# A gated scan and two feed-forward networks on one core: the scan steps of a pair of blocks released at given TensorE steps, planned in finer pieces, with a planner that may wait shortly for a step

## The chip, the cores and the metric

One core of a Trainium2 chip. The metric is the device time of one execution in microseconds (us).

## The reference

```python
sig = 1.0 / (1.0 + np.exp(-f_logit))                 # batch 2, sequence 6080, width 256
f = lower_bound + (1.0 - lower_bound) * sig
for t in range(S):                                   # per batch, from h = 0
    h = f[:, t] * h + (1.0 - f[:, t]) * x[:, t]
    y[:, t] = h
x = y.reshape(B * S, D)                              # 12160 tokens
h = np.maximum(x @ w_in, 0.0); x = h * h @ w_out     # network 1, hidden width 2048
h = x @ w_in2; g = np.where(h > 0, h, np.exp(np.minimum(h, 0)) - 1)
out = g @ w_out2                                     # network 2, hidden width 2048
```
The weights arrive as float64 and are brought to float32 on the chip.

## The kernel before, in words

**Blocks and slots.** The 12160 tokens are cut into 24 blocks (the first of 384 tokens, the others of 512), taken two by two as pairs. For one network, one block and one of 8 groups of 256 hidden units there is one *slot* of work, 384 slots in all. Network 1 of one pair (16 slots) alternates with network 2 of the pair two places earlier (16 slots). Counted from 0, slots 0 to 31 are network 1 of the first two pairs, 32 to 47 network 2 of the first pair, 48 to 63 network 1 of the third pair, 64 to 79 network 2 of the second pair, and so on: a *cycle* has 32 slots.

**One slot.** float32 products are made of three rounded ones (a value is split into a rounded high part and its residual). TensorE does `first` (3 of 7 block products of the input side, L611), then the output products of the slot three before (`out`, L710), then `later` (the other 4, L611). ScalarE copies three quarters of the PSUM result to SBUF (`snap`, L639) between `first` and `later`. VectorE adds the pieces (L647, L654, L642, L650), ScalarE takes the first block (L657) and the activation: relu and square for network 1; for network 2 two steps L667 and L670, after which VectorE forms the elu (L673). ScalarE rounds the result (L678), VectorE makes its residual (L683, tile `g`): this is the last thing that `out` of the slot waits for. In the text "the residual of slot 64" is that slot's L683. The first four blocks of network 1 use plain products (L625) instead of L611.

**The scans.** Each block is scanned in two halves, each a chain of steps: two loads on the SP queue (`fs`, `xs`), a tanh on ScalarE (L545), on VectorE two transposes (L550), the gate (two instructions L559), the scan's input (L562), the scan itself (two instructions L576) and the copy of the last column for the next half (L578). The buffers `fs`, `xs`, `fT` and `xT` exist once, `F` (the scanned block) twice. From `F` the *parts* are made (L484, L488, L492, rounded L500 or L502, residual L508), written to `xA` or `xB`, which TensorE's `first` reads. The scans of a pair can therefore run while network 2 of another pair is in TensorE.

**The order.** Every step is given to `Order.add` with its engine, an assumed duration, a due time, and what it reads and writes. `Order.run` plays the program through with these durations: at each turn the engine that is free first takes, of its steps that are ready at that moment, the one that is due soonest. The order so found is written out, engine by engine, as the program; on the chip each engine works through its list in that order and waits by semaphores. The order of TensorE's steps (`pe_order`) is written out beforehand. In the kernel before, a half's gate is one step, its scan with the copy is one step, and each may start as soon as its buffers are free.

## Time and profile before

| | before |
|---|---|
| median of 3 runs | 2113.92 us (2113.29 to 2114.46) |
| profiled execution, its own time | 2113.18 us |
| profiled execution, span from first to last instruction | 2111.4 us |
| TensorE products busy | 2041.2 us (97%) |
| TensorE weight loads busy | 1925.7 us (91%) |
| VectorE busy | 1717.8 us (81%) |
| ScalarE busy | 1692.7 us (80%) |

The profiled execution is one run of its own; 1.8 us of its time lie outside the span. Busy shares are means over the whole program: where an engine waits is seen in the rows by stretch.

### The profile page before, as it was taken

To read this page: it belongs to the slowest core of one execution; us is meant where nothing else is said; L and a number is where in the kernel's file an instruction comes from. 1 tells how busy PE (TensorE), PEld (TensorE's weight loads), DVE (VectorE), ACT (ScalarE), POOL (GpSimd) and SP (SyncE) were. 2 spreads that over 40 slices of the span, in tenths; PEclk is the share of its full clock that TensorE was granted. 3 is DMA by queue.
4 is the path that set the end of the run, shared out by engine and by line. 5 is a ranking of instruction groups with operands and counts; after the bars stand their busy time and mean duration, and the time that the engine had idled before them with its cause. 6 is when DMAs were issued, how large, how long until landed. Compare 5 with 4: busy or idle time off the path is not lost.

```text
span 2111.4 us, 36876 instructions
## 1 busy us (share of the span) xinstructions
PE 2041.2 (97%) x14640; PEld 1925.7 (91%) x14640; DVE 1717.8 (81%) x2833; ACT 1692.7 (80%) x2146; POOL 0.2 (0%) x4
## 2 busy tenths in 40 slices
PE   3999899999999999999999999999999999999998
PEld 2888889999899899999999989989999998999998
DVE  6977986986987887798698698789879859867886
ACT  5877787887788888788788888878878878878886
POOL 0000000000000000000000000000000000000000
PEclk8999999999999999999999999999999999999999
DMA  7877442432433433333243243333334324323231
GB/s 214 230 261 246 152 149 88 136 130 83 135 118 108 123 113 128 120 105 123 92 142 131 85 138 103 123 118 108 122 117 117 128 88 128 125 90 128 88 108 38
DMA packets 207539, 268.08 MB, mean 127 GB/s; under 512 B 110984, under 2 KB 135944, under 8 KB 207368
## 3 DMA queue, kind: packets, MB, share of 16 engines
q1 hardware_dynamic: 206784, 265.21, 39.9%
q8 instruction: 115, 1.88, 0.4%
q10 hardware_dynamic: 584, 0.53, 0.1%
q14 instruction: 56, 0.46, 0.1%
HBM read 221.91 MB, written 43.78 MB: 126 GB/s over the span
## 4 chain that ended last, share of the span: by engine, by line
PE 71%; DVE 20%; ACT 4%; DMA 2%; issue 2%; SPq 1%; DVEq 0%; ACTq 0%
PE acc L710 38%; PE pc L611 30%; DVE g L683 4%; PE pc L625 4%; DVE r L654 2%; DVE F L576 2%; DVE r L673 2%; DVE s L642 1%; DVE r L650 1%; DVE s L647 1%; DVE fT L559 1%; DMA xs<-in_x_dram 1%; DVE fT L550 1%; DVE xA L508 1%; DVE xT L562 1%
## 5 line engine op out<-in xcount | busy, mean ns | idle before, releaser
L710 PE MATMUL acc<-wo,g 128*128 128x256 f32 x4560 | 584.4, 283 | 20.2 <-DVE g L683 19.9
L710 PEld LDWEIGHTS acc<-wo,g 128*128 128x128 f32 x4560 | 561.3, 188 | 25.9 <-DVE g L683 25.2
L710 PE MATMUL acc<-g,wo 128*128 128x512 f32 (+1 forms) x2304 | 552.2, 389 | 0.0
L611 PE MATMUL pc<-xA,ws 128*128 128x256 f32 (+1 forms) x3696 | 486.1, 280 | 7.1 <-ACT s L639 7.1
L683 DVE TENSOR_TENSOR g<-r,g 128x1024 fp32r<-128x1024 f32 (+1 forms) x384 | 463.6, 1207 | 35.4 <-ACT g L678 34.3
L710 PEld LDWEIGHTS acc<-g,wo 128*128 128x128 f32 x2304 | 420.7, 188 | 78.1
L611 PE MATMUL pc<-xB,ws 128*128 128x256 f32 x3696 | 487.0, 281 | 3.9 <-ACT s L639 3.9
L611 PEld LDWEIGHTS pc<-xA,ws 128*128 128x128 f32 x3696 | 462.1, 188 | 17.0 <-ACT s L639 11.2
L611 PEld LDWEIGHTS pc<-xB,ws 128*128 128x128 f32 x3696 | 463.4, 188 | 11.0 <-ACT s L639 4.6
L678 ACT ACTIVATE g<-r 128x1024 fp32r<-128x1024 f32 (+1 forms) x384 | 403.1, 1050 | 58.3 <-DVE r L673 51.5
L647 DVE TENSOR_TENSOR s<-pc,s 128x256 f32<-128x256 f32 (+1 forms) x352 | 147.7, 420 | 283.5 <-PE pc L611 283.3
L639 ACT ACTIVATE s<-pc 128x768 f32<-128x768 f32 (+1 forms) x352 | 283.1, 804 | 48.8 <-PE pc L611 48.0
L673 DVE SCALAR_TENSOR_TENSOR r<-e,r 128x1024 f32<-128x1024 f32 (+1 forms) x192 | 231.2, 1204 | 22.7 <-ACT e L670 22.7
L654 DVE TENSOR_TENSOR r<-pc,s 128x512 f32<-128x512 f32 (+1 forms) x352 | 241.0, 685 | 7.7 <-ACT r L657 2.6
L657 ACT ACTIVATE r<-pc 128x256 f32<-128x256 f32 (+1 forms) x352 | 134.0, 381 | 112.5 <-DVE r L654 66.4
L660 ACT ACTIVATE r<-r 128x768 f32<-128x768 f32 x160 | 135.6, 847 | 105.3 <-DVE r L650 105.3
L667 ACT ACTIVATE e<-r 128x1024 f32<-128x1024 f32 (+1 forms) x192 | 201.2, 1048 | 19.0 <-DVE r L650 14.6
L663 ACT ACTIVATE r<-r 128x1024 f32<-128x1024 f32 (+1 forms) x192 | 202.1, 1053 | 5.4
L670 ACT ACTIVATE e<-e 128x1024 f32<-128x1024 f32 (+1 forms) x192 | 201.6, 1050 | 5.0
L642 DVE TENSOR_TENSOR s<-s 128x256 f32<-128x256 f32 (+1 forms) x352 | 147.4, 419 | 9.3 <-ACT s L639 0.7
L650 DVE TENSOR_TENSOR r<-s 128x256 f32<-128x256 f32 (+1 forms) x352 | 147.0, 418 | 0.0
L625 PE MATMUL pc<-xA,ws 128*128 128x384 f32 (+1 forms) x192 | 44.0, 382 | 23.2 <-DVE xA L502 22.9
(49 smaller groups left out, 849.5 us busy)
## 6 DMA issues: line engine op xcount, KB each, us to landing
ws<-wd SPq DMA_DIRECT2D x176, 896.0 KB, 5.0
out_dram<-o SPq DMA_DIRECT2D x47, 256.0 KB, 2.4
fs<-in_f_logit_dram SPq DMA_DIRECT2D x184, 64.0 KB, 2.4
xs<-in_x_dram SPq DMA_DIRECT2D x184, 64.0 KB, 2.8
xd<-o SPq DMA_DIRECT2D x46, 256.0 KB, 3.4
F<-xd SPq DMA_DIRECT2D x46, 256.0 KB, 5.0
st<-in_moe_w_out_dram SPq DMA_DIRECT2D x16, 512.0 KB, 4.9
wd<-wp SPq DMA_DIRECT2D x24, 256.0 KB, 4.7
```

The costliest lines, as they stand in the source:

```text
L611: nc.tensor.matmul(t["pc"][:, c], lhsT=ws[:, p, w], rhs=x_t[m, b][:, r, v], start=(which is FIRST_PRODUCTS and q == 0 and c in (1, 2)), st ...
L639: nc.scalar.activation(t["s"], t["pc"][:, 1:4], AF.Copy)
L642: nc.vector.tensor_tensor(t["s"][:, 1], t["s"][:, 1], t["s"][:, 2], op=ALU.add)
L647: nc.vector.tensor_tensor(t["s"][:, 0], t["pc"][:, 0], t["s"][:, 0], op=ALU.add)
L654: nc.vector.tensor_tensor(t["c"][:, 1:3], t["pc"][:, 2:4], u, op=ALU.add)
L663: nc.scalar.activation(t["r"], t["r"], AF.Square)
L667: nc.scalar.activation(t["e"], t["r"], AF.Relu, scale=-1.0)
L670: nc.scalar.activation(t["e"], t["e"], AF.Exp, scale=-1.0)
L673: nc.vector.scalar_tensor_tensor(t["r"], t["e"], 1.0, t["r"], op0=ALU.subtract, op1=ALU.max)
L678: nc.scalar.activation(t["g"][:, 0], t["r"], AF.Copy)
L683: nc.vector.tensor_tensor(t["g"][:, 1], t["r"], t["g"][:, 0].bitcast(F32), op=ALU.subtract)
L710: nc.tensor.matmul(a, lhsT=u, rhs=v, start=clear and k == 0, stop=two and k == 2, skip_group_check=True)
```

## The change

Three things, and no instruction of another kind. For the third pair on (`b >= 2 * BEHIND`), the transposes of the four scan halves of a pair may be planned no sooner than TensorE begins `first` of the slots 15, 11, 8 and 4 places before the pair's first slot (`SPREAD`); this binds the planner alone, and adds no semaphore on the chip. The two gate instructions, the two scan instructions and the carry copy of a half are five steps instead of two, and the two instructions that make the gate's constants (`bound`) are a step of their own that only needs `lb`. And the planner may choose a step that becomes ready up to 0.2 us after the moment (`HOLD`), if it is due sooner than those that are ready. TensorE's order stays word for word as it was; VectorE has 2832 instructions instead of 2835, ScalarE 2157 instead of 2154 (some roundings move between them).

```diff
--- before.py
+++ after.py
@@ -25,6 +25,7 @@
 AGE = 10.0
 ROW = 1 / 2185
 START = 12.0
+SPREAD = (15, 11, 8, 4)
 
 BUFS = {
     "fs": 1, "xs": 1, "fT": 1, "xT": 1, "F": 2, "xA": 1, "xB": 1, "ws": 4, "wp": 3, "r": 3, "e": 1,
@@ -53,6 +54,7 @@
 
     SAME, CROSS, LOAD = 0.13, 0.22, 2.4
     RATE, AHEAD = 240.0, 2.0
+    HOLD = 0.2
     SLACK = 0.3
 
     def __init__(self):
@@ -61,8 +63,9 @@
         self.readers = {}
         self.users = {}
         self.first = {}
-
-    def add(self, engine, us, due, what, reads=(), writes=(), other=None, kb=0):
+        self.after = set()
+
+    def add(self, engine, us, due, what, reads=(), writes=(), other=None, kb=0, after=None):
@@ -83,11 +86,14 @@
                 self.users.setdefault(k[:2], []).append(n)
                 self.first.setdefault(k[:2], n)
         needs.discard(n)
+        if after is not None:
+            self.after.add((after, n))
         self.steps.append([engine, us, due, what, needs, other, kb])
+        return n
 
     def run(self):
         steps = self.steps
-        after = set()
+        after = self.after
         for (tag, k), n in self.first.items():
             steps[n][4].update(self.users.get((tag, k - BUFS[tag]), ()))
             if k and self.first[tag, k - 1] != n:
@@ -125,7 +131,8 @@
                 if not r:
                     continue
                 t0 = max(free[e], min(r.values()))
-                n = min((n for n, t in r.items() if t <= t0), key=lambda n: steps[n][2])
+                n = min((n for n, t in r.items() if t <= t0 + self.HOLD), key=lambda n: steps[n][2])
+                t0 = max(t0, r[n])
                 if best is None or t0 < best[0]:
                     best = (t0, e, n)
             t0, e, n = best
@@ -422,6 +429,7 @@
             ["DVE", dve(CE), sign, [st], [a]],
         ]
         if i == 0:
+            steps[0][4].append(("lb",))
             order.add(*steps[0][:2], -20.0, *steps[0][2:])
             del steps[0]
         if m == 1 and kind == 0:
@@ -527,7 +535,7 @@
         ])
-    def add_scan(i, b, h, due):
+    def add_scan(i, b, h, due, after=None):
         n = sizes[b] // 2
         t0 = starts[b] + h * n
         u = n_unit[0, b]
@@ -550,23 +558,24 @@
                 nc.vector.transpose(t[dst].rearrange("p c (n i) -> p n c i", i=32), t[src])
             return go
 
-        def gate(e):
-            if i == 0:
-                nc.vector.tensor_scalar(ga, lb, -0.5, 0.5, op0=ALU.mult, op1=ALU.add)
-                nc.vector.tensor_scalar(gb, lb, 0.5, 0.5, op0=ALU.mult, op1=ALU.add)
-            f = t["fT"]
-            for c in range(KD):
+        def gate(c):
+            def go(e):
+                f = t["fT"]
                 nc.vector.tensor_scalar(f[:, c], f[:, c], ga[:, c : c + 1], gb[:, c : c + 1], op0=ALU.mult, op1=ALU.add)
+            return go
+
+        def bound(e):
+            nc.vector.tensor_scalar(ga, lb, -0.5, 0.5, op0=ALU.mult, op1=ALU.add)
+            nc.vector.tensor_scalar(gb, lb, 0.5, 0.5, op0=ALU.mult, op1=ALU.add)
 
         def feed(e):
             nc.vector.scalar_tensor_tensor(t["xT"], t["fT"], 1.0, t["xT"], op0=ALU.subtract, op1=ALU.mult)
 
-        def scan(e):
-            if h == 0:
-                F_t[0, b] = new("F", [P, NX + 1, HB])[:, :, :n]
-            a, z = block_slots(0, b)[h]
-            for c in range(KD):
-                y = F_t[0, b][:, (a, z)[c]]
+        def scan(c):
+            def go(e):
+                if h == 0 and c == 0:
+                    F_t[0, b] = new("F", [P, NX + 1, HB])[:, :, :n]
+                y = F_t[0, b][:, block_slots(0, b)[h][c]]
                 done = 0
                 while done < n:
                     s = (t0 + done) % S
@@ -575,6 +584,10 @@
                     d = slice(done, done + m)
                     nc.vector.tensor_tensor_scan(y[:, d], t["fT"][:, c, d], t["xT"][:, c, d], init, ALU.mult, ALU.subtract)
                     done += m
+            return go
+
+        def carry_on(e):
+            a, z = block_slots(0, b)[h]
             nc.vector.tensor_copy(carry, F_t[0, b][:, a : z + 1 : z - a, n - 1])
 
         fs, xs, fT, xT = (("fs", i), ("xs", i), ("fT", i), ("xT", i))
@@ -583,11 +596,13 @@
             ["SP", 1.9, load("fs", ff), (), [fs], None, n],
             ["SP", 1.9, load("xs", xf), (), [xs], None, n],
             ["ACT", act(N), tanh, (), [fs]],
-            ["DVE", dve(N), turn("xs", "xT"), [xs], [xT]],
-            ["DVE", dve(N), turn("fs", "fT"), [fs], [fT]],
-            ["DVE", 2 * dve(n, True), gate, (), [fT]],
+            ["DVE", dve(N), turn("xs", "xT"), [xs], [xT], None, 0, after],
+            ["DVE", dve(N), turn("fs", "fT"), [fs], [fT], None, 0, after],
+            *([["DVE", 0.2, bound, [("lb",)], [("bound",)]]] if i == 0 else []),
+            *(["DVE", dve(n, True), gate(c), [("bound",)], [fT]] for c in range(KD)),
             ["DVE", dve(N), feed, [fT], [xT]],
-            ["DVE", dve(N) + 0.3, scan, [fT, xT] + [("F", u, 0)] * h, [("F", u, h), ("carry",)]],
+            *(["DVE", dve(n) + 0.1, scan(c), [fT, xT, ("carry",)] + [("F", u, 0)] * h, [("F", u, h)]] for c in range(KD)),
+            ["DVE", 0.1, carry_on, [("F", u, h)], [("carry",)]],
         ])
@@ -847,13 +862,16 @@
             use.update({(m, b, g): use[m, bs[0], g] for g in range(KG)})
 
     made = {}
+    n_first = {}
     n_scan = 0
     for kind, s in pe_order:
         m, b, g = s
         if kind == "first":
             if m == 0 and g == 0:
                 for h in range(2):
-                    add_scan(n_scan, b, h, in_due[s] - 6.0)
+
+                    k = slots.index((0, b - b % 2, 0)) - SPREAD[b % 2 * 2 + h]
+                    add_scan(n_scan, b, h, in_due[s] - 6.0, n_first[slots[k]] if b >= 2 * BEHIND else None)
                     n_scan += 1
                 add_parts(0, b, [("F", n_unit[0, b], h) for h in range(2)], in_due[s])
             elif g == 0:
@@ -862,7 +880,9 @@
             made[s] = add_slot(slots.index(s), m, b, g, use[s])
         if kind != "later" or not plain(m, b):
             one = made[s][0][kind]
-            order.add(one[0], one[1], one[2], *one[3:])
+            n = order.add(one[0], one[1], one[2], *one[3:])
+            if kind == "first":
+                n_first[s] = n
         if kind == "later":
             chain(out_due[s], made[s][2])
         if kind == "first":
```

VectorE's list from the residual of slot 64 to that of slot 65 and a little beyond, in the second pair's network 2 (`r`, `e`, `s`, `pc`, `g` are a slot's tiles, `fT`, `xT`, `xs`, `fs`, `F`, `carry` the scan's). Before:

```order
L683 TENSOR_TENSOR g<-r,g 128x1024
L576 SCALAR_TENSOR_TENSOR F<-fT,carry,xT 128x256 x2
L578 COPY carry<-F 128x2
L647 TENSOR_TENSOR s<-pc,s 128x256
L550 STREAM_TRANSPOSE xT<-xs 128x8x2x32
L673 SCALAR_TENSOR_TENSOR r<-e,r 128x1024
L654 TENSOR_TENSOR r<-pc,s 128x512
L642 TENSOR_TENSOR s<-s 128x256
L650 TENSOR_TENSOR r<-s 128x256
L550 STREAM_TRANSPOSE fT<-fs 128x8x2x32
L683 TENSOR_TENSOR g<-r,g 128x1024
L559 TENSOR_SCALAR fT<-fT,ga,gb 128x256 x2
```

The same place in the change:

```order
L698 TENSOR_TENSOR g<-r,g 128x1024
L564 TENSOR_SCALAR fT<-fT,ga,gb 128x256
L572 SCALAR_TENSOR_TENSOR xT<-fT,xT 128x512
L662 TENSOR_TENSOR s<-pc,s 128x256
L688 SCALAR_TENSOR_TENSOR r<-e,r 128x1024
L669 TENSOR_TENSOR r<-pc,s 128x512
L657 TENSOR_TENSOR s<-s 128x256
L665 TENSOR_TENSOR r<-s 128x256
L585 SCALAR_TENSOR_TENSOR F<-fT,carry,xT 128x256
L698 TENSOR_TENSOR g<-r,g 128x1024
```

Between the two residuals stood a whole scan, its copy and two transposes of the next half; now there are one gate, the scan's input and one scan instruction.

VectorE's list from the residual of slot 78 to that of slot 79, the last of network 2 in the same cycle. Before:

```order
L683 TENSOR_TENSOR g<-r,g 128x1024
L647 TENSOR_TENSOR s<-pc,s 128x256
L508 TENSOR_TENSOR xB<-F,xB 128x768
L673 SCALAR_TENSOR_TENSOR r<-e,r 128x1024
L642 TENSOR_TENSOR s<-s 128x256
L654 TENSOR_TENSOR r<-pc,s 128x512
L650 TENSOR_TENSOR r<-s 128x256
L484 TENSOR_TENSOR F<-F 128x512
L683 TENSOR_TENSOR g<-r,g 128x1024
```

In the change:

```order
L698 TENSOR_TENSOR g<-r,g 128x1024
L585 SCALAR_TENSOR_TENSOR F<-fT,carry,xT 128x256 x2
L492 TENSOR_TENSOR F<-F 128x512
L688 SCALAR_TENSOR_TENSOR r<-e,r 128x1024
L662 TENSOR_TENSOR s<-pc,s 128x256
L591 COPY carry<-F 128x2
L669 TENSOR_TENSOR r<-pc,s 128x512
L657 TENSOR_TENSOR s<-s 128x256
L665 TENSOR_TENSOR r<-s 128x256
L496 TENSOR_TENSOR F<-F 128x256
L500 TENSOR_TENSOR F<-F 128x256
L698 TENSOR_TENSOR g<-r,g 128x1024
```

The scan of the pair's last half, with three instructions of the parts behind it, now stands in this slot.

VectorE's list at the program's start, up to the second weight tile (`a`, `st` and `ws` belong to the weights, `lb`, `ga` and `gb` to the gate's constants). Before:

```order
L382 SCALAR_TENSOR_TENSOR a<-a,st 128x512
L550 STREAM_TRANSPOSE xT<-xs 128x6x2x32
L550 STREAM_TRANSPOSE fT<-fs 128x6x2x32
L385 SCALAR_TENSOR_TENSOR a<-st,a 128x512
L555 TENSOR_SCALAR ga<-lb 128x2
L556 TENSOR_SCALAR gb<-lb 128x2
L559 TENSOR_SCALAR fT<-fT,ga,gb 128x192 x2
L562 SCALAR_TENSOR_TENSOR xT<-fT,xT 128x2x192
L408 TENSOR_TENSOR ws<-a,ws 128x512
L576 SCALAR_TENSOR_TENSOR F<-fT,xT 128x192 x2
L578 COPY carry<-F 128x2
L382 SCALAR_TENSOR_TENSOR a<-a,st 128x512
```

In the change:

```order
L568 TENSOR_SCALAR ga<-lb 128x2
L569 TENSOR_SCALAR gb<-lb 128x2
L558 STREAM_TRANSPOSE fT<-fs 128x6x2x32
L558 STREAM_TRANSPOSE xT<-xs 128x6x2x32
L564 TENSOR_SCALAR fT<-fT,ga,gb 128x192 x2
L572 SCALAR_TENSOR_TENSOR xT<-fT,xT 128x2x192
L585 SCALAR_TENSOR_TENSOR F<-fT,xT 128x192 x2
L591 COPY carry<-F 128x2
L389 SCALAR_TENSOR_TENSOR a<-a,st 128x512
L392 SCALAR_TENSOR_TENSOR a<-st,a 128x512
L411 CAST ws<-a 128x512
L389 SCALAR_TENSOR_TENSOR a<-a,st 128x512
```

The first scan half now stands ahead of the first weight tile's two steps and of its residual.

## Rows read from the trace of the kernel before

**Rows 1.** The page's first part: busy us, share of the span, instructions.
```profile
PE 2041.2 (97%) x14640; PEld 1925.7 (91%) x14640; DVE 1717.8 (81%) x2833; ACT 1692.7 (80%) x2146; POOL 0.2 (0%) x4
```
**Rows 2.** The waits from 375 to 1785 us: total us, times, longest.
```profile
PE acc L710 <- DVE g L683: 14.7, 18, 1.0
...
DVE g L683 <- ACT g L678: 12.2, 32, 0.8
...
PE pc L611 <- ACT s L639: 5.1, 9, 0.6
```
**Rows 3.** One cycle's window: us; busy of PE, PEld, DVE, ACT, POOL; clock; DMA.
```profile
380.00:552.30 172.30, 170.11 (x1250) 161.47 (x1249) 141.27 (x232) 140.94 (x178) 0.00 (x0) 1.00 0.37 117
```
**Rows 4.** TensorE's timeline, the cycle's last wait: start us, us, instruction [idle before].
```profile
404.45 2.90 PE L710 MATMUL acc<-wo,g 128*128 128x256 f32 x22 [0.98 <-DVE g L683]
```
**Rows 5.** TensorE's timeline, `first` of successive slots: network 2, then network 1.
```profile
419.33 1.23 PE L611 MATMUL pc<-xA,ws 128*128 128x256 f32 x9
...
424.69 1.23 PE L611 MATMUL pc<-xB,ws 128*128 128x256 f32 x9
...
337.40 1.22 PE L611 MATMUL pc<-xB,ws 128*128 128x256 f32 x9
...
342.61 1.22 PE L611 MATMUL pc<-xA,ws 128*128 128x256 f32 x9
```
**Rows 6.** VectorE's timeline between the residuals of slots 64 and 66.
```profile
395.97 0.70 DVE L550 STREAM_TRANSPOSE fT<-fs 128x512 f32<-128x512 f32 x1
396.60 1.18 DVE L683 TENSOR_TENSOR g<-r,g 128x1024 fp32r<-128x1024 f32 x1
397.70 0.73 DVE L559 TENSOR_SCALAR fT<-fT,ga,gb 128x256 f32<-128x256 f32 x2
...
398.67 0.68 DVE L562 SCALAR_TENSOR_TENSOR xT<-fT,xT 128x512 f32<-128x512 f32 x1
399.27 1.22 DVE L673 SCALAR_TENSOR_TENSOR r<-e,r 128x1024 f32<-128x1024 f32 x1
400.41 0.69 DVE L654 TENSOR_TENSOR r<-pc,s 128x512 f32<-128x512 f32 x1
...
401.68 1.39 DVE L576 TENSOR_TENSOR_SCAN F<-fT,carry,xT 128x256 f32<-128x256 f32 x2
...
403.18 1.22 DVE L683 TENSOR_TENSOR g<-r,g 128x1024 fp32r<-128x1024 f32 x1
```
**Rows 7.** Slots without scan work: VectorE's waits in networks 2 and 1, slot 73's residual and `out`.
```profile
435.63 0.42 DVE L647 TENSOR_TENSOR s<-pc,s 128x256 f32<-128x256 f32 x1 [1.28 <-PE pc L611]
...
438.49 1.23 DVE L683 TENSOR_TENSOR g<-r,g 128x1024 fp32r<-128x1024 f32 x1
...
441.88 1.36 PE L710 MATMUL acc<-wo,g 128*128 128x256 f32 x10
...
520.33 0.42 DVE L647 TENSOR_TENSOR s<-pc,s 128x256 f32<-128x256 f32 x1 [2.08 <-PE pc L611]
```
**Rows 8.** The waits from 200 to 305 us.
```profile
PE pc L611 <- ACT s L639: 5.8, 5, 1.6
...
PE acc L710 <- DVE g L683: 3.7, 6, 0.8
```
**Rows 9.** The timeline at the start, up to the second block's first products.
```profile
9.18 0.69 DVE L382 SCALAR_TENSOR_TENSOR a<-a,st 128x512 int32<-128x512 int32 x1 [8.32 <-ACT st L379]
...
33.94 0.96 DVE L683 TENSOR_TENSOR g<-r,g 128x768 fp32r<-128x768 f32 x1 [0.50 <-ACT g L678]
35.95 0.96 DVE L683 TENSOR_TENSOR g<-r,g 128x768 fp32r<-128x768 f32 x1 [1.06 <-ACT g L678]
...
44.02 1.22 DVE L508 TENSOR_TENSOR xB<-F,xB 128x1024 fp32r<-128x1024 f32 x1
...
45.29 4.45 PE L625 MATMUL pc<-xB,ws 128*128 128x512 f32 x11 [1.37 <-DVE xB L508]
```
**Rows 10.** The same view of the stretch in which TensorE waits for the second block.
```profile
32.32:43.12 10.80, 0.01 (x2) 0.00 (x1) 9.14 (x17) 7.43 (x11) 0.00 (x0) 0.63 0.99 308
```

## The prediction

> **What bounds the kernel now.** I read the page first. TensorE's products are busy for 2041.2 of 2111.4 us, and no other engine is above 81% [rows 1]. So a change of order can only win time in which TensorE stands still, and the waits say where that is. Through the regular part of the program it waits 18 times for a residual from VectorE and 9 times for ScalarE's copy [rows 2]: 9 cycles, each with the same three waits. The timeline puts them at one place, where network 1 of a pair ends and network 2 of another begins (the last and longest of one cycle is [rows 4]). The reader is to see that nothing else in the cycle stops TensorE.
>
> How much a cycle loses is read from the lengths of slots that nothing disturbs: 424.69 - 419.33 = 5.36 us in network 2 (5.37 over several) and 342.61 - 337.40 = 5.21 us in network 1 [rows 5]. 16 of each are 169.3 us, and the cycle takes 172.3 [rows 3]: 3.0 us lost. The idle time alone is 172.3 - 170.1 = 2.2; the rest is in products that the trace shows as busy while they wait for their weights.
>
> The Trainium skill ("Perfetto Trace Analysis", Identifying the Most-Contended Engine) says that the busy share of the products is a poor measure of the room left, and that the busy share of the weight loads is a better one. By that the room in a cycle is 172.3 - 161.5 = 10.8 us [rows 3], and nine cycles without it would end at 2113 - 97 = 2016. The undisturbed slots do not bear out that number, since they have gaps between weight loads too; I go by their lengths.
>
> Why VectorE is late there: from the residual of slot 64 to that of slot 66 it has no idle time at all [rows 6]. I price its work by the distance from one start to the next, not by durations, which overlap: a residual 1.10 us, an elu 1.14, the wide addition with the two small ones after it 1.27, the gate pair with a slot's first addition 0.97, the scan's input 0.60, a transpose 0.63, two scan instructions with the copy 1.50 [rows 6]. A network 2 slot without scan work is then 3.85 us, and a half of a scan 4.0 us. Priced so, VectorE's list for slots 60 to 66 of the kernel before holds 6.1, 5.6, 6.0, 5.4, 6.1, 6.5 and 6.5 us, 42.2 in all; TensorE needs 4 x 5.21 + 3 x 5.37 = 37.0 for these slots. VectorE falls 5.2 us behind. It starts with a lead of about 2.2 us (slot 73's residual ends at 439.72, and TensorE takes it up at 441.88 [rows 7]). 5.2 - 2.2 = 3.0, the loss found above, so this arithmetic can be trusted for the list of the change. In quiet slots VectorE waits 1.28 us for TensorE in network 2 and 2.08 in network 1 [rows 7]: the room is there, elsewhere.
>
> **The regular cycles.** The list of the change has all four halves of a pair's scan in slots 64 to 79, the steps of a half spread over two or three slots, and four or so slots between one half and the next. The same prices give, for slots 60 to 66, 5.1, 2.4, 3.7, 5.5, 5.4, 5.5 and 4.6 us, 32.2 against TensorE's 37.0: never behind by more than 0.3. The whole of network 2 (slots 64 to 79) has 16 x 3.85 = 61.6 us of slot work, 4 x 4.0 = 16.0 of scans and 4.5 of parts, 82.1 against 16 x 5.37 = 85.9. It fits, with 3.8 us to spare. The heaviest slot is the last one, 79, with 6.5 us (the residual, the scan of two instructions, L492 and its two followers stand in it): 1.2 us over TensorE's slot, under the lead of 2.2, and slots 80 and 81 hold 4.4 and 4.3 against 5.2, so it is made good. No instruction is added, and the 0.2 us that the planner may wait is no wait on the chip, where an engine goes on as soon as its semaphores allow. ScalarE's fullest slot of the change holds 5.3 us, priced the same way, under 5.37. The loads of the next half have those slots, some 20 us, to land in. So all three waits go: 9 x 3.0 = 27.0 us, and at least 9 x 2.2 = 19.8 if the hidden part stays.
>
> **From 200 to 305 us**, network 2 of the first pair, VectorE also prepares the last weights. TensorE's idle time there is 5.8 + 3.7 = 9.5 us [rows 8]; with the hidden part in the same ratio as in a cycle (3.0 to 2.2) some 12.7 us are lost. Between the residuals of slots 32 and 46, VectorE's list shrinks from 81.2 to 72.4 us, 8.8 less. By slot 49 only 1.3 of this is left (92.4 against 91.1): 7.5 us come back in three slots of network 1, which have 2.08 us of room each [rows 7], 6.2 in all, so 1.3 are late. And slot 32 itself holds 8.3 instead of 4.3 us (weight work), for which I take off 1. Gain 8.8 - 1.3 - 1.0 = 6.5 us; at worst 2 (if the refilled slots wait again), at best the 12.7.
>
> **The start.** TensorE does three slots of the first block and then stands until 45.29, when the second block's residual is there [rows 9]. VectorE begins at 9.18 and comes to that residual at 44.02. Ahead of it its list loses two steps of a weight tile, one weight residual (0.60 each), two slot residuals of 768 columns (0.87 each) and one rounding (0.46), and gains two roundings (0.36 each): 3.3 us less work. With the two slot residuals go the waits of 0.50 and 1.06 us in front of them [rows 9], as long as nothing else is late there. So 3.3 to 4.9; I take 4.5, because the first scan half also begins a little sooner, its tanh now coming before a weight step on ScalarE. What could eat it is the loads: the 16 DMA engines are 0.99 busy in that stretch [rows 10], so the lower end is 0; the upper is 7 (both halves sooner and their waits gone). The clock matters little: its mean in that stretch is 0.63 [rows 10], that is, it falls from 2.4 to 1.2 GHz while TensorE stands, and TensorE stands there in the change as well; in the regular cycle it is 1.00 [rows 3], 2.4 GHz throughout, so those waits cost nothing beyond themselves.
>
> The sum: 2113.18 - 27.0 - 6.5 - 4.5 = 2075.2 in the profiled execution's own time. The median of the runs is 0.7 above it: **2076 us**, 1.8% faster.
>
> **The rivals.** (1) *Only the regular cycles gain.* The DMA share of 0.99 [rows 10] speaks for it: the second block's loads land when they did, and the transition keeps its loss, since the same work is only pushed into slots 47 to 49. 2113.9 - 27.0 = 2087.
> (2) *The waits have another cause than VectorE's order.* The skill (same page, Optimization Strategy) says that the same bubble repeating on the engine that should be full can mean too few buffers for the next tile. That would leave the order without effect: PSUM's two `pc` buffers would hold TensorE whatever VectorE does, and 27.0 would shrink to the start's 4.5 with part of the transition, some 2105. Against it: TensorE's waits end with a residual or a copy that is itself behind VectorE [rows 2], VectorE has no idle time there [rows 6], and in quiet slots the same buffers do without a wait [rows 5, 7]. A milder form, in which each cycle keeps a third to a half of its loss, gives 2085 to 2090.
> (3) *VectorE becomes the bound of network 2; slower.* Its 82.1 us now lie in 85.9. Each slot has a chain between engines (copy, activation, elu, rounding, residual), and every wait of VectorE inside it, which idle room covered so far, now counts. In the kernel before VectorE waits 12.2 us in nine cycles for ScalarE's rounding, the longest such wait, under 0.1 us a slot of network 2 [rows 2]. TensorE would lose in a cycle 16 w - 3.8 - 2.2 for a wait of w us a slot: nothing up to w = 0.38, 3.0 (today's loss) at 0.56, and with the gains at the start and the transition (11 us, 1.2 a cycle) slower than before from w = 0.64 on. At 0.8, 16 x 0.8 - 6.0 = 6.8 a cycle: 2076 + 9 x 6.8 = 2137. For it: the sum is tight. Against it: the waits would have to grow sevenfold, a full list leaves less to wait for, as [rows 6] show, and the scan steps stand just before the elu, where VectorE would wait for ScalarE anyway.
> (4) *No change*: the waits move to other slots at the same price, 2114.
>
> **The numbers.** Forecast 0.60 (2068 to 2083); rival 1 and the milder form of 2, 0.24 (2083 to 2093); the rest of rival 2, 0.07 (2093 to 2110); no change 0.03; slower 0.06. Range 2068 to 2093, with 0.84 in it: its lower end has the start at 7 and the transition almost gone, its upper end three quarters of the cycles' gain alone. A measurement tells 0.2% (4 us) from no change: faster 0.91, within 0.2% 0.03, slower 0.06.
>
> **What would show it.** Right: the cycle falls from 172.3 to about 169.3 us, the 18 and 9 waits are gone, VectorE's waits for TensorE spread evenly over network 2; TensorE starts the second block at about 41 instead of 45.3 us; idle time of TensorE between 200 and 305 falls to about 4 us. Wrong: VectorE waits for ScalarE (elu or residual) in most slots of network 2 and TensorE for the residual in slots 76 to 80; or a transpose waits for a load. The prediction fails if slot 79's residual comes more than 2.2 us late in every cycle.

## The result

The changed kernel takes **2084.62 us** (median of 4 runs, 2083.75 to 2086.09) against 2113.89 (4 runs, 2113.29 to 2114.46): a ratio of 0.9863, 95% interval 0.9847 to 0.9878, 1.4% faster. The forecast was 2076 with a range of 2068 to 2093. The profiled execution took 2083.75 us, 29.4 less than that of before.

The page's first part for the changed kernel answers to [rows 1]: TensorE's products are busy for 6.7 us less; the other 22.7 of the 29.4 us are idle time that went.

```profile
span 2082.0 us, 36897 instructions
...
PE 2034.5 (98%) x14640; PEld 1925.6 (92%) x14640; DVE 1732.3 (83%) x2830; ACT 1697.1 (82%) x2149; POOL 0.2 (0%) x4
```

The waits of the changed kernel through its regular part (total us, times, longest), which answer to [rows 2]. No row of TensorE is left. VectorE waits for TensorE as it did before (211.6 us, 127 times, up to 2.4 in the same view of the kernel before); the waits of about 2.1 us are those of network 1.

```profile
engine line waited for: us in total, times, longest us
DVE s L662 <- PE pc L626: 187.4, 114, 2.1
ACT s L654 <- PE pc L626: 81.4, 109, 1.4
ACT r L675 <- DVE r L665: 59.7, 72, 0.8
```

Inside one network 2 (slots 64 to 79, VectorE's part of it from 374 to 460 us) VectorE waits for TensorE for 0.8 us in all, in two slots. Over the nine cycles these waits fell from 46.9 to 8.9 us: VectorE's room in network 2 is nearly used up, without loss to TensorE.

```profile
DVE s L662 <- PE pc L626: 0.8, 2, 0.7
```

One cycle of the changed kernel as a window (us; busy time of each engine), to be laid beside [rows 3]: 169.3 us, with TensorE busy in all of it.

```profile
365.40:534.70 169.30, 169.30 (x1250) 161.40 (x1249) 142.17 (x231) 141.40 (x178) 0.00 (x0) 1.00 0.38 119
```

The start of TensorE's second block in the changed kernel, to be laid beside [rows 9]. It begins at 41.29 instead of 45.29; its wait for the residual is 0.51.

```profile
39.98 0.80 PE L640 MATMUL pc<-xB,ws 128*128 128x512 f32 x1 [10.09 <-ACT xB L508]
41.29 5.00 PE L640 MATMUL pc<-xB,ws 128*128 128x512 f32 x11 [0.51 <-DVE xB L516]
46.13 0.51 PE L725 MATMUL acc<-g,wo 128*128 128x384 f32 x2
```

TensorE's waits of the changed kernel from 200 to 305 us, which answer to [rows 8]. The waits for VectorE's residual fell from 3.7 to 1.0; the five for ScalarE's `snap` are all still there, and two new ones add 1.9. The idle time is 8.5 us, where the prediction expected about 4.

```profile
PE pc L626 <- ACT s L654: 5.6, 5, 1.7
PE pc L626 <- issue: 1.2, 1, 1.2
PE acc L725 <- DVE g L698: 1.0, 2, 0.8
PE pc L626 <- DVE r L669: 0.7, 1, 0.7
```

Where the 29.4 us came from is read from the starts of `out` in both traces. The first `out` comes 3.44 us sooner; from `out` 31 to 51 (the transition) it takes 0.93 less; from `out` 51 to 380 another 26.7 less, all of it in the nine cycles; from `out` 380 to 383 it takes 2.15 **more**; what follows the last `out` gives 0.5 back.

### The profile page after: what moved, and what is told of

Read it like the earlier page. It is cut to its first block, busy times and chain, and to the rows that moved or that the text cites. A ratio compares the mean times of both kernels' runs of the same rounds, so it can differ in the third digit from the quotient of the medians.

```text
span 2082.0 us, 36897 instructions
## 1 busy us (share of the span) xinstructions
PE 2034.5 (98%) x14640; PEld 1925.6 (92%) x14640; DVE 1732.3 (83%) x2830; ACT 1697.1 (82%) x2149; POOL 0.2 (0%) x4
## 4 chain that ended last, share of the span: by engine, by line
PE 93%; DVE 4%; ACT 1%; DMA 1%; issue 0%; SPq 0%; DVEq 0%; ACTq 0%
PE acc L725 49%; PE pc L626 40%; PE pc L640 4%; DVE g L698 1%; DVE r L688 1%; DVE r L669 0%; DMA fs<-in_f_logit_dram 0%; DVE F L585 0%; ACT g L693 0%; DMA a<-rd 0%; DVE s L662 0%; ACT s L654 0%; SPq L328 0%; ACT e L682 0%; DVE r L665 0%
## 5 line engine op out<-in xcount | busy, mean ns | idle before, releaser
L626 PEld LDWEIGHTS pc<-xB,ws 128*128 128x128 f32 x3696 | 463.6, 188 | 11.6 <-ACT s L654 4.2
L693 ACT ACTIVATE g<-r 128x1024 fp32r<-128x1024 f32 (+1 forms) x384 | 402.1, 1047 | 15.6 <-DVE r L688 8.6
L669 DVE TENSOR_TENSOR r<-pc,s 128x512 f32<-128x512 f32 (+1 forms) x352 | 241.8, 687 | 9.3
L682 ACT ACTIVATE e<-r 128x1024 f32<-128x1024 f32 (+1 forms) x192 | 202.0, 1052 | 15.0 <-DVE r L665 6.5
L672 ACT ACTIVATE r<-pc 128x256 f32<-128x256 f32 (+1 forms) x352 | 133.4, 379 | 79.5 <-DVE r L669 66.6
L585 DVE TENSOR_TENSOR_SCAN F<-fT,carry,xT 128x256 f32<-128x256 f32 (+2 forms) x94 | 65.7, 728 | 0.3
```

Of the source, the lines that this page charges most:

```text
L626: nc.tensor.matmul(t["pc"][:, c], lhsT=ws[:, p, w], rhs=x_t[m, b][:, r, v], start=(which is FIRST_PRODUCTS and q == 0 and c in (1, 2)), st ...
L669: nc.vector.tensor_tensor(t["c"][:, 1:3], t["pc"][:, 2:4], u, op=ALU.add)
L682: nc.scalar.activation(t["e"], t["r"], AF.Relu, scale=-1.0)
L693: nc.scalar.activation(t["g"][:, 0], t["r"], AF.Copy)
```

## The experiments

All medians are over runs beside the kernel before, which stood at 2113.3 to 2114.1 us. Columns from the traces: start of the first `out`; time from `out` 31 to 51; a cycle ((start of `out` 348 less that of 60) / 9); time from `out` 380 to 383.

| kernel | median us (range) | first | 31 to 51 | cycle | end |
|---|---|---|---|---|---|
| before | 2113.89 | 49.57 | 111.77 | 172.32 | 11.63 |
| the change | 2084.62 (2083.75 to 2086.09) | 46.13 | 110.84 | 169.35 | 13.78 |
| 1 no release | 2084.27 (2082.16 to 2085.36) | 45.67 | 109.00 | 169.46 | 13.78 |
| 2 release alone | 2096.54 (2095.95 to 2097.22) | 49.06 | 112.92 | 170.32 | 11.63 |
| 3 single steps alone | 2107.76 (2106.68 to 2108.66) | 48.97 | 111.88 | 171.66 | 11.63 |
| 4 waiting alone | 2091.93 (2089.64 to 2091.99) | 45.96 | 108.59 | 170.24 | 13.78 |
| 5 no waiting at the end | 2083.16 (2081.07 to 2084.05) | 46.16 | 110.75 | 169.45 | 12.08 |
| 6 loads planned faster | 2090.57 (2088.31 to 2092.60) | 44.92 | 112.01 | 169.56 | 11.63 |
| 7 measured lead | 2108.76 (one run) | 45.20 | 110.82 | see text | 13.78 |
| 8 waiting 0.4 | 2082.76 (2081.84 to 2086.52) | 43.86 | 106.70 | 169.35 | 11.63 |
| 9 GpSimd | 2085.24 (2084.64 to 2085.76) | 45.84 | 112.69 | 169.50 | 12.07 |
| 10 waiting 1.0 | 2189.49 (one run) | 42.06 | 121.46 | 180.44 | 11.63 |
| 11 GpSimd, 0.35 | 2085.91 (2085.70 to 2086.04) | 44.79 | 114.77 | 169.35 | 12.08 |
| 12 less weight work | 2080.76 (2080.42 to 2082.49) | 46.32 | 107.36 | 169.44 | 12.07 |

Kernels 1 and 5 have the same order up to the last slots and still differ by 1.8 us between `out` 31 and 51. 1.5 of that arise at one place, the `later` of slot 47. TensorE waits there equally long in both; behind the wait the clock granted to it is 1.00 (2.4 GHz) in kernel 1 and 0.50 (1.2 GHz) for 3.4 us in kernel 5. TensorE's timeline and a window (the number before the DMA share is the clock), kernel 1 and then kernel 5:

```profile
281.11 1.68 PE L626 MATMUL pc<-xB,ws 128*128 128x256 f32 x12 [1.91 <-ACT s L654]
281.10:284.50 3.40, 3.39 (x28) 3.39 (x29) 2.91 (x7) 2.98 (x4) 0.00 (x0) 1.00 0.89 281
```
```profile
282.23 2.64 PE L626 MATMUL pc<-xB,ws 128*128 128x256 f32 x12 [1.92 <-ACT s L654]
282.60:286.00 3.40, 3.40 (x19) 3.40 (x18) 1.94 (x5) 1.97 (x3) 0.00 (x0) 0.50 0.89 297
```

So a difference of that size there can be the clock alone. In the traces before, of the change and of kernels 1, 3, 4 and 12 the clock does not fall between 50 us and the end of the regular part; in those of kernels 2, 5, 6, 8, 9 and 11 it falls once or twice between 200 and 305 us, each time about the end of a wait of TensorE of 1.8 to 3.7 us.

### Which part of the change does it (1 to 4)

**1, the change without the release:**

```diff
-                    add_scan(n_scan, b, h, in_due[s] - 6.0, n_first[slots[k]] if b >= 2 * BEHIND else None)
+                    add_scan(n_scan, b, h, in_due[s] - 6.0, None)
```

> The changed kernel with the release of the scan halves taken out (no step waits for a slot of TensorE); the single gate and scan steps and the planner's 0.2 us of waiting stay. Theory A (the release is what spreads the scans and so takes the waits of the cycles): the cycle goes back to about 172 us and the time to 2085 + 27 = 2112. Theory B (what counts is only how far VectorE's list falls behind TensorE; priced as in the prediction, with 5.29 us a slot taken off and never under zero, the list of this kernel falls at most 1.4 us behind in a regular cycle, against 3.2 before and 1.2 in the change, and the kernel before shows that about 1.7 us are absorbed): no loss in the cycles, cycle 169.3, time 2085, between 2081 and 2090 for what start and transition may do.

Measured 2084.27, cycle 169.46: theory A falls, theory B's 2085 came. The release, the part of the change with a table of its own, can be left out.

**2, the release alone** (gate and scan one step each, no waiting):

```diff
-    HOLD = 0.2
+    HOLD = 0.0
-            *(["DVE", dve(n, True), gate(c), [("bound",)], [fT]] for c in range(KD)),
+            ["DVE", 2 * dve(n, True), lambda e: [gate(c)(e) for c in range(KD)], [("bound",)], [fT]],
...
-            *(["DVE", dve(n) + 0.1, scan(c), [fT, xT, ("carry",)] + [("F", u, 0)] * h, [("F", u, h)]] for c in range(KD)),
-            ["DVE", 0.1, carry_on, [("F", u, h)], [("carry",)]],
+            ["DVE", dve(N) + 0.3, lambda e: [scan(0)(e), scan(1)(e), carry_on(e)], [fT, xT] + [("F", u, 0)] * h, [("F", u, h), ("carry",)]],
```

> The kernel before with the release alone: gate and scan are one step for each half as before, and the planner doesn't wait for steps due sooner (0.2 us back to 0). Theory A: the cycles win their 27 us by the release alone, cycle 169.3, time 2114 - 27 = 2087 with the start as before. Theory B: the list falls up to 2.1 us behind, in three places of a cycle, of which about 0.6 us a cycle is over the 1.7 that are absorbed: cycle about 169.9, and with the start as before (3.4 us of the change's gain missing) and without the change's loss of 1.7 us at the end some 2085 + 5 + 3.4 - 1.7 = 2092.

Measured 2096.54, further up than theory B's 2092: a cycle takes 170.32 and not 169.9, which makes 3.8 of the 4.5 us.

**3, the single steps alone:** the change with `None` for the release and `HOLD = 0.0`.

> The kernel before with single steps for gate, bound, scan and copy, but neither release nor 0.2 us of waiting. Both theories: the cycles gain nothing (the list falls up to 3.4 us behind, 3.0 us a cycle over 1.7): cycle 172.3. What it tells is where the 3.4 us of the start and the 1.7 us lost at the end come from: if the start's gain belongs to the single steps, the first slot of the second block starts near 40 us instead of 45.3 and the time is about 2110; if it belongs to the waiting, 2114.

Measured 2107.76. The start did not move (48.97), so its gain is not theirs; but a cycle gains 0.7 us, where both theories had none, and that makes the 6 us.

**4, the waiting alone:** the two edits of 1 and 2 together, but with `HOLD = 0.2`.

> The kernel before with one number of the planner changed alone: an engine may wait up to 0.2 us for a step that is due sooner. Neither release nor single steps. Theory A: no spread, so the cycles keep their loss: 2114, cycle 172.3. Theory B: the list falls 1.2 to 2 us behind, some 0.35 us a cycle over the 1.7 that are absorbed: cycle 169.6, time about 2114 - 24 = 2090, and 2 us more if the loss at the end comes with the waiting.

Measured 2091.93. Theory B's sum (2090 and 2 for the end) was hit in part by luck: a cycle lost 0.9 us and not 0.3, and the start (3.6) and the transition (3.2), which the sum left out, made up for it. Kernels 2 and 4 keep `bound` as a step of its own; the start of kernel 2 is 0.5 us sooner than before.

TensorE's waits of kernels 2, 3 and 4, in this order, from 375 to 1785 us (beside 14.7 in 18 for the residual and 5.1 in 9 for `snap` before [rows 2]):

```profile
PE acc L724 <- DVE g L697: 2.6, 8, 0.3
```
```profile
PE acc L725 <- DVE g L698: 8.3, 26, 0.5
```
```profile
PE acc L724 <- DVE g L697: 4.4, 9, 0.6
```

A cycle loses, over 169.35 us: before 2.97, single steps 2.31, release 0.97, waiting 0.89, waiting and single steps 0.11, all three 0. The lists, priced as in the prediction and with a lead of 1.7 us, had said beforehand 3.0 for single steps, 0.6 for the release, 0.35 for the waiting and 0 for waiting and single steps: the ranking is right, and no figure is off by more than 0.7, which for the two small ones is half of what was measured and more. So each of release and waiting cures most of a cycle, and they don't add up. Release with single steps and without the waiting was not run. The start is the waiting's alone (45.96 with it, 49.06 and 48.97 with the others), and so is the loss at the end (13.8 against 11.6 us). One number of the planner, 0 to 0.2, is worth about 22 of the 29 us.

### Is it the lead? (7 and 10)

**7, the changed kernel with extra VectorE work**, growing from cycle to cycle:

```diff
         def low_part(e):
+            for _ in range(3 * ((i - 72) // 32) if i % 32 == 8 and 72 <= i < 352 else 0):
+                nc.vector.tensor_tensor(spare, spare, spare, op=ALU.mult)
             nc.vector.tensor_tensor(t["g"][:, 1], t["r"], t["g"][:, 0].bitcast(F32), op=ALU.subtract)
```

> The changed kernel with extra work for VectorE that the result doesn't need: in front of the residual of slots 104, 136, ... 328 stand 3, 6, ... 24 small multiplications of 128x128 (0.2 us each by the price of other additions), so that each cycle has 0.6 us more than the last, from none to 4.8. Slot 72 of network 2 and its neighbours hold 5.1 to 5.2 us, so almost nothing of it is made good before network 1. Theory B: what VectorE is late is absorbed up to the lead of about 1.5 to 1.7 us, and all above it is lost: cycles of 169.3 with 0 to 1.2 us, then 169.5, 170.1, 170.7, 171.3, 171.9, 172.5: the time about 10 us above the changed kernel's. Rival R (the waits have another cause, and TensorE holds more in reserve, or none): no cycle longer, or every cycle longer by all that is added, 21.6 us in all.

Each small multiplication took about 0.32 us from start to start, not 0.2, so the doses were larger. VectorE's timeline of this kernel at the third dose (nine multiplications; start us, us), the wait that it makes on TensorE, and the sum of all such waits:

```profile
933.02 2.90 DVE L700 TENSOR_TENSOR spare<-spare 128x128 f32<-128x128 f32 x9
935.84 1.22 DVE L701 TENSOR_TENSOR g<-r,g 128x1024 fp32r<-128x1024 f32 x1
```
```profile
937.11 1.10 PE L728 MATMUL acc<-wo,g 128*128 128x256 f32 x7 [0.33 <-DVE g L701]
```
```profile
PE acc L728 <- DVE g L701: 16.7, 6, 5.2
```

| added us | 0 | 0.86 | 1.83 | 2.82 | 3.80 | 4.78 | 5.76 | 6.73 | 7.72 |
|---|---|---|---|---|---|---|---|---|---|
| TensorE's wait | 0 | 0 | 0 | 0.33 | 1.31 | 2.29 | 3.27 | 4.24 | 5.23 |
| cycle longer by | 0 | 0 | 0.1 | 1.1 | 2.1 | 3.1 | 4.8 | 6.8 | 8.0 |
| clock after the wait | 1.00 | 1.00 | 1.00 | 1.00 | 1.00 | 1.00 | 0.50, 3.4 us | 0.50, 6.8 us | 0.50, 6.8 us |

From 1.83 to 4.78 us the cycle grows by what is added, less **1.69 us** (2.82 - 1.13, 3.80 - 2.11, 4.78 - 3.08): that is the lead. The visible wait is what is added less 2.49; the 0.8 between them is lost in products that the trace shows as busy, the hidden part of which the prediction spoke. Laid beside the trace of the change, that 0.8 has two parts. At the third dose 0.58 us are lost in the late `out` itself (0.33 visible), so the lead at that place is 2.82 - 0.58 = 2.24 us, the 2.2 of the prediction. The other 0.55 us are lost behind it, in steps of 0.1 to 0.2 us in the products of slots 172 to 178. Rival R falls.

From 5.76 us on more is lost than the 1.69 allow, by 0.7 to 2.0 us. In these three cycles, and in no other, the granted clock falls to 0.50 (1.2 GHz) shortly before the wait ends. The window behind the wait with 4.78 us added, and then the one in which the clock is down with 5.76:

```profile
1281.02:1287.02 6.00, 6.00 (x50) 6.00 (x51) 5.93 (x11) 3.48 (x5) 0.00 (x0) 1.00 0.05 10
1453.90:1457.30 3.40, 2.87 (x13) 2.87 (x14) 3.33 (x7) 0.38 (x1) 0.00 (x0) 0.50 0.00 0
```

**10, waiting of 1.0 us** (`HOLD = 1.0`, with the edits of 5, below):

> As the kernel without waiting at the end, with 1.0 us of waiting in place of 0.2: the arithmetic of the lists where it says slower. Theory B: the list falls so far behind in each cycle that 7.6 us a cycle stand over a lead of 1.7; cycle about 177, nine of them 68 us, and 4 to 6 us more between slots 31 and 51: about 2155. Rival (the waiting is good in itself, since steps due sooner go first): 2080 to 2090.

Measured 2189.49, cycle 180.44: 11.1 us lost in each, not 7.6, but on the side that the lists gave and the rival excluded. TensorE's idle time alone is 8.0 us a cycle, near the 7.6 of the lists. Its longest wait is at the `first` of the third slot of network 1; in every cycle the granted clock falls to 0.50 before it ends, for 6.8 or 10.3 us. Timeline of TensorE and the window behind the wait, one cycle:

```profile
482.19 2.26 PE L626 MATMUL pc<-xA,ws 128*128 128x256 f32 x9 [6.26 <-issue]
479.30:486.10 6.80, 3.90 (x18) 3.94 (x19) 6.73 (x12) 3.52 (x4) 0.00 (x0) 0.50 0.37 92
```

So part of what the lists missed is the clock: half of the 3.90 us of products in this window, some 2 us, is an estimate of its price. The rest was not taken apart. The transition (121.46) lost 11 us, not 4 to 6. Priced by the rows, slot 79 holds some 11 us of VectorE's work here: a planner that so often waits for the step due sooner leaves the scans to the end of network 2.

### The end (5)

```diff
-                n = min((n for n, t in r.items() if t <= t0 + self.HOLD), key=lambda n: steps[n][2])
+                n = min((n for n, t in r.items() if t <= t0 + (self.HOLD if t0 < self.until else 0.0)), key=lambda n: steps[n][2])
...
+    order.until = in_due[slots[-8]]
```

This on top of 1, so without the release.

> The changed kernel without the release (as in the first experiment), and the planner's 0.2 us of waiting switched off for the last eight slots alone. Theory: the loss of 2.1 us between slots 381 and 383, which only the three kernels with the waiting show, comes from ScalarE's order there: the cycle and the rest stay, 2084.3 - 2.1 = 2082. Rival: the two orders end alike because the same work is left over after the last product: 2084.

ScalarE's timeline in the changed kernel and then in this one, at slots 382 and 383:

```profile
2062.61 1.06 ACT L682 ACTIVATE e<-r 128x1024 f32<-128x1024 f32 x1 [0.38 <-DVE r L688]
2063.58 1.04 ACT L693 ACTIVATE g<-r 128x1024 fp32r<-128x1024 f32 x1
```
```profile
2063.79 1.05 ACT L693 ACTIVATE g<-r 128x1024 fp32r<-128x1024 f32 x1
2064.74 1.05 ACT L682 ACTIVATE e<-r 128x1024 f32<-128x1024 f32 x1
```

With waiting, ScalarE does the next slot's activation L682 ahead of the rounding L693 that the slot being finished needs. TensorE's wait for L693 falls from 1.7 to 0.6 us, and the end from 13.78 to 12.08: 1.7 of the 2.15 us are this order. The medians of kernels 1 and 5 are 1.1 apart and their ranges overlap; it is the trace that shows the gain.

### The transition (6, 8, 9, 11 and 12)

**6, loads planned at 280 instead of 240 GB/s** (`RATE`; with the edits of 5), which moves preparation of weights into earlier slots:

> As the kernel without waiting at the end, with the planner's rate for loads at 280 instead of 240 GB/s: 12 us of VectorE's list, preparation of weights, move from slots 32 to 51 into slots 16 to 31, where TensorE doesn't wait. Theory V (the 9 to 12 us lost between slots 31 and 51 in every kernel so far are VectorE's list being longer than TensorE's time there): the losses after slot 38 go, those of slots 32 to 38 stay, since their list is the same: some 4 to 5 us won, 2077.5. Rival D (the loads are the limit, they moved 246 GB/s there): VectorE waits for loads in slots 16 to 31 instead, and the time is 2082 or longer. Rival L (single slots with lumps and the order on ScalarE make the loss, not the sum): 2080 to 2082.

Slower, 2090.57. TensorE's, ScalarE's and VectorE's timelines of this kernel show the new stalls:

```profile
204.04 4.80 PE L626 MATMUL pc<-xA,ws 128*128 128x192 f32 x21 [3.26 <-ACT s L654]
212.53 2.14 PE L626 MATMUL pc<-xA,ws 128*128 128x192 f32 x17 [0.54 <-ACT s L654]
```
```profile
201.22 1.06 ACT L693 ACTIVATE g<-r 128x1024 fp32r<-128x1024 f32 x1
202.82 0.63 ACT L553 ACTIVATE fs<-fs 128x512 f32<-128x512 f32 x1 [0.55 <-DVE a L340]
203.36 0.63 ACT L654 ACTIVATE s<-pc 128x576 f32<-128x576 f32 x1
211.31 0.63 ACT L409 ACTIVATE wo<-a 128x512 fp32r<-128x512 f32 x1 [7.32 <-DVE a L392]
```
```profile
201.75 0.29 DVE L337 TENSOR_TENSOR a<-a 128x128 f32<-128x128 f32 x1 [1.70 <-DMA a<-rd]
```

TensorE's 3.3 us are for the `snap` of slot 32, which stands at 203.36 behind a rounding and a tanh in ScalarE's list, the tanh held up for 0.55 us by VectorE, which had waited 1.70 us for a load. Next ScalarE stands for 7.32 us at the rounding of a weight that VectorE has not formed yet, with the `snap` of slot 33 behind it; TensorE waits another 0.5 us for that. From shortly before the ends of the waits at slots 32 and 36 the granted clock is 0.50 for 6.8 us each. This is the profiled execution, 2092.6 us, mean clock 0.993; two of the four runs are at 2088.3 and 2088.9 with 0.997, so some 4 us of the longer runs go with the clock. Rival D fits better than V, but the stall is made by the order as much as by the load, so the run doesn't decide what the transition loses to VectorE.

**8, as 6 with waiting of 0.4:**

> As the kernel with loads planned faster, with 0.4 us of waiting in place of 0.2. Theory B: the list of the cycles is now never more than 0.8 us behind, so that the last 0.12 us a cycle go (1 us in all); slots 32 to 51 hold some 3 us more than at 0.2: between 2076 and 2080. Rival: more waiting keeps VectorE idle on the chip as well, and the time rises above 2082.

2082.76: the cycles' last 0.1 us go, as the lists say. From `out` 31 to 51 it is the shortest of all, but only because its stall, of the kind of 6, lies at slot 32, whose `later` comes ahead of `out` 31: TensorE waits 3.6 us there, the clock is at 0.50 behind it, and the slots up to `out` 31 lose 6.2 us. From the first `out` to `out` 51 it takes 274.4 us against the change's 272.3.

**9, subtractions of the weights on GpSimd** (with the edits of 5):

```diff
-            nc.vector.tensor_tensor(t[x].bitcast(F32R), t[x], t["w" + x].bitcast(F32), op=ALU.subtract)
+            nc.gpsimd.tensor_tensor(t[x].bitcast(F32R), t[x], t["w" + x].bitcast(F32), op=ALU.subtract)
...
-            ["DVE", dve(CE), low_part, [w], [key]],
+            ["POOL", 1.5, low_part, [w], [key]],
```

The subtractions of network 2's output weights move in the same way.

> As the kernel without waiting at the end, with 32 subtractions of the preparation of weights (0.6 us each) given to GpSimd, which has nothing else to do; loads and their rate stay. Theory S (the loss between slots 31 and 51 is VectorE's list against TensorE's own pace slot by slot, whose slots there last 2.9 to 7.0 us; the losses of seven kernels there, 8.8 to 13.1 us, stand within 2 us of what falls behind by more than 1 us in that sum): the sum is 6.8 us here against 9.0 without GpSimd, so some 2 to 4 us won there, time 2079 to 2081. Rival L (order on ScalarE makes the loss): no change, 2083. Rival G (GpSimd's instructions are slow or hold VectorE up, and what waits for them comes late): slower than 2085.

2085.24, rival G. GpSimd's and VectorE's timelines of this kernel:

```profile
155.75 2.20 POOL L415 TENSOR_TENSOR wo<-a,wo 128x512 fp32r<-128x512 f32 x1 [1.09 <-DVE wo L411]
160.81 3.60 POOL L354 TENSOR_TENSOR a<-a,wp 128x512 fp32r<-128x512 f32 x2 [2.85 <-DMA F<-xd]
```
```profile
155.59 1.22 DVE L698 TENSOR_TENSOR g<-r,g 128x1024 fp32r<-128x1024 f32 x1
156.72 1.78 DVE L389 SCALAR_TENSOR_TENSOR a<-a,st 128x512 int32<-128x512 int32 x1
...
160.93 2.32 DVE L698 TENSOR_TENSOR g<-r,g 128x1024 fp32r<-128x1024 f32 x1
```

A residual that begins 0.12 us after a GpSimd instruction takes 2.32 us, one that begins 0.16 before it 1.22, and then GpSimd's takes 2.20 instead of 1.3. Such meetings eat into what VectorE saves; one of them, an addition of 1.42 us instead of 0.28, stands ahead of the longest wait of TensorE in the transition (2.6 us at slot 36), after which the clock falls to 0.50 for 3.4 us. That the meetings are all of the loss is not shown.

**11, as 9 with waiting of 0.35:**

> As the kernel with 32 subtractions on GpSimd, with 0.35 us of waiting in place of 0.2. By the lists no cycle falls more than 1 us behind, and the sum for slots 31 to 51 is 6.6: 1 us in the cycles and little else, 2078 to 2081; the fastest so far if GpSimd costs nothing.

2085.91: a miss by 5 us, in the transition again; the cycles, at 169.35, won what was expected. TensorE waits 3.7 us at the `first` of slot 50, which begins 0.1 us after VectorE's addition L669 of slot 48 ends; two scan instructions stand ahead of that in VectorE's list.

**12, less work for VectorE, same order** (with the edits of 5; it leaves work out):

```diff
         def magnitude(e):
+            if m == 1:
+                return
...
         def sign(e):
+            if m == 1:
+                return
...
     def weight_sums(q, a):
+        nc.vector.tensor_copy(q, a)
+        return
...
         def low_part(e):
+            return
```

The last of these is the `low_part` of the kept parts.

> As the kernel without waiting at the end, in the same order on every engine, but VectorE leaves out part of the preparation of weights: the two integer steps for network 2's tiles, the subtractions of the kept parts, and one copy stands for the four additions of the sums (so the weights that the products use are not the true ones; their number, sizes and loads stay). 5.3 us less fall behind by the slot by slot sum for slots 31 to 51 (3.7 in place of 9.0 over a lead of 1 us). Theory S (VectorE's list against TensorE's pace makes the loss there): about 5 us won between slots 31 and 51, 10 us lost become about 5, time 2078. Rival L (the loss comes from the order in which ScalarE meets its waits, and from loads): 2082 to 2084, the loss stays at 9 to 11 us.

2080.76, 2.4 us below kernel 5 and not 5, with ranges that overlap; against kernel 1, whose clock did not fall either, the transition is 1.6 us shorter. That lies between theory S and rival L. TensorE's waits of this kernel from 200 to 305 us are one row:

```profile
PE pc L633 <- ACT s L661: 6.0, 5, 1.9
```

The waits for VectorE's residual are all gone; the five for `snap` are as long as in the kernel before (5.8 [rows 8]). So they don't come from the weight work on VectorE. TensorE's timeline of the changed kernel at one of them, then ScalarE's:

```profile
255.88 1.24 PE L626 MATMUL pc<-xB,ws 128*128 128x256 f32 x9
258.76 1.70 PE L626 MATMUL pc<-xB,ws 128*128 128x256 f32 x12 [1.65 <-ACT s L654]
```
```profile
255.38 1.06 ACT L693 ACTIVATE g<-r 128x1024 fp32r<-128x1024 f32 x1 [1.42 <-DVE r L688]
257.68 0.33 ACT L672 ACTIVATE r<-pc 128x192 f32<-128x192 f32 x1 [1.25 <-DVE r L669]
257.91 0.80 ACT L654 ACTIVATE s<-pc 128x768 f32<-128x768 f32 x1
```

And at slot 47, where ScalarE is ready in time, in the same order:

```profile
280.99 1.68 PE L626 MATMUL pc<-xB,ws 128*128 128x256 f32 x12 [0.90 <-ACT s L654]
```
```profile
280.13 0.81 ACT L654 ACTIVATE s<-pc 128x768 f32<-128x768 f32 x1 [0.58 <-PE pc L626]
```

At both places the nine products of `first` are followed at once by the twelve of `later` of the same slot. `snap` stands between the two. With ScalarE ready at once the wait is 0.90 us, as at slot 47, and 0.74 at the two slots of the small block (32 and 36). Three of the one and two of the other are 4.2 of the 5.6 to 6.0 us. The remaining 1.4 to 1.8 are ScalarE's list: at slot 43 `snap` stands behind L672, which waits 1.25 us for an addition on VectorE (L669). Everywhere else an `out` of some 2.8 to 3.0 us lies between `first` and `later` and hides `snap`. In the whole program `first` and `later` of one slot are neighbours at five places, slots 32, 36, 39, 43 and 47, in the kernel before, in the changed one and in this one, and there stand the five waits. The same five are there in the other kernels too. That they go with the places is shown, that another TensorE list would cure them is not: it was not tried, and neither was `snap` ahead of L672.

## Why the prediction was right, and where it was not

**The regular cycles: right in size.** 27.0 forecast, 26.7 measured; the 18 and 9 waits are gone and a cycle is 169.3 us. Slot 79's residual was no trouble: it ends 0.7 us before its `out` begins (466.08 and 466.78). Three things in that step were off. The lead of 2.2 us is right at the late `out` itself (2.24 in kernel 7), but 1.69 when it is counted in lost time; the changed list's heaviest slot is 1.2 over, so this cost nothing. The list of slots 60 to 66 falls 0.45 us behind by the prediction's own numbers, not 0.3, which changes nothing. And the credit was wrong: the prediction spoke of the halves being spread, which is the release, and passed the waiting by with the remark that it is no wait on the chip. It isn't, but it decides which step comes first in VectorE's list. Without release the same gain is there (kernel 1): by the planner's rule a scan step no longer slips in ahead of a slot's step that is due sooner and ready within 0.2 us. Priced with the same rows, the list of kernel 1 did tell so, before it ran. And one sign did not come: VectorE's waits for TensorE are not spread over network 2 but nearly gone from it.

**The start: 4.5 forecast, 3.4 measured.** TensorE takes up the second block's products 4.0 us sooner (41.29 against 45.29), with its wait for the residual down by 0.86. Another 0.56 us is lost behind that: the eleven products up to the first `out` took 4.84 us instead of 4.28, at a granted clock of 0.50, which is 1.2 GHz throughout, against 0.58 before. The windows, before and then the change:

```profile
45.29:49.57 4.28, 4.28 (x11) 3.38 (x12) 1.93 (x3) 0.61 (x2) 0.00 (x0) 0.58 0.61 186
41.29:46.13 4.84, 4.84 (x11) 3.84 (x12) 4.81 (x8) 0.90 (x2) 0.00 (x0) 0.50 0.45 150
```

"The clock matters little" holds for this trace of the change, where the clock fell nowhere else before the end; kernels 5, 6, 7 and 10 show that a wait can cost the clock too.

**The transition: the step that failed.** The prediction put all 9.5 us of TensorE's idle time there down to VectorE being late, 12.7 with the hidden part, and took 6.5 of it for won. 0.93 was won, a figure that the clock alone could move by some 1.5 (kernels 1 and 5), but not to 6.5. Of the 9.5 us, 5.8 are the five waits for `snap` at places where TensorE's list leaves nothing to hide it; the change doesn't touch that list, and kernel 12 keeps them with VectorE's weight work lightened. Only the 3.7 us for the residual were VectorE's, and these fell to 1.0, as they should: counted from `out` 31, the change is 3.4 us ahead at `out` 45. By `out` 50 it has lost 2.5 of that again, where the prediction had taken off 1.3 for VectorE's refilled slots. The two new waits are at the `first` of slots 50 and 51. At slot 50 the view names no cause ("issue"); VectorE's timeline shows that the addition L669 of slot 48 ends 0.1 us before, behind a scan:

```profile
294.55 1.29 PE L626 MATMUL pc<-xA,ws 128*128 128x256 f32 x9 [1.16 <-issue]
```
```profile
291.66 1.39 DVE L585 TENSOR_TENSOR_SCAN F<-fT,carry,xT 128x256 f32<-128x256 f32 x2
...
293.77 0.68 DVE L669 TENSOR_TENSOR r<-pc,s 128x512 f32<-128x512 f32 x1
```

The name of the awaited tile in [rows 8] would have told the two kinds apart. (9.5 us in the ratio of 3.0 to 2.2 are 13.0, not 12.7.)

**The end: not forecast.** 2.15 us more, 1.7 of them by ScalarE's order under the waiting (kernel 5).

**The rivals.** That only the cycles gain, 2087, came nearest. Of its reason the second half was seen, work pushed into slots just behind the transition; that the loads are behind it is not. Buffers are excluded: with the same buffers the cycles lose nothing. VectorE as the bound of network 2 did not come, since TensorE waits nowhere in the cycle; but with 1 us a cycle of waits for TensorE left to VectorE there, it is not far.

## What to carry to other kernels

When an engine's list makes another wait, price the list slot by slot against the pace of the one that waits, and measure the lead by adding known work: here 1.7 us; what lies beyond it is lost one for one up to 4.8 us of added work, and beyond that the clock fell as well. Test the parts of a change apart before believing in the one that it is named after: here a planner's tolerance of 0.2 us gave 22 of 29 us, and 1.0 us made the kernel 76 us slower than before. Before waits of one stretch are added up, look at what stands next to each in the waiting engine's own list; five of eleven here stayed when VectorE's weight work was lightened. Look at the granted clock behind each long wait before a miss is put down to the arithmetic. None of the versions beats the change clearly: the best that computes the same, with release left out and either no waiting at the end or 0.4 us of waiting with loads planned faster, are at 2083, and their intervals (0.9836 to 0.9863 and 0.9841 to 0.9868) overlap with the change's.

## What the runs showed of the hardware

About the end of a wait of TensorE in the middle of the program the granted clock fell in some cases to 0.50 (1.2 GHz): not with a wait of 1.91 us in kernel 1, but with one of 1.92 in kernel 5; not with 2.29 in kernel 7, but with 3.27, 4.24 and 5.23 there and with the longest wait of every cycle in kernel 10. The same twelve products took 2.64 us in kernel 5 and 1.68 in kernel 1.

GpSimd took 1.3 us for a subtraction of 128x512 that costs VectorE 0.6 from start to start. Where the two met, the one that came second took about 1 us longer (the timelines of kernel 9); VectorE's transposes (0.70 us with and without GpSimd beside them) and its additions with one input in PSUM (L669, 0.69 both ways) were not slowed. Of the conversions in kernel 9, those of 0.42 us had begun before GpSimd's instruction; one of 128x1024 that began 0.2 us after it took 1.79 us instead of 0.69:

```profile
113.01 1.79 DVE L510 CAST xB<-F 128x1024 fp32r<-128x1024 f32 x1
```

The Trainium skill ("SBUF — State Buffer", SBUF: two separate sides) says that the two share a pair of ports that is locked for a whole instruction, also against VectorE's instructions with two SBUF inputs; the rows of the residual agree, with about 1.1 us of waiting for an instruction of 1.3.
